# A new instruction order for an attention and mixer kernel, from a planner that counts two readers of one PSUM tile as serial, with the first loads on one queue

## The chip, the cores and the metric

The kernel runs on one core of one Trainium2 chip. The metric is the device time of one execution in microseconds (us). Every kernel ran at least four times, in rounds beside the kernel before on the same chip. A ratio of two kernels is the mean time of the one's fast runs over that of the other's fast runs of the same rounds, so it is not quite the ratio of the medians that stand beside it. The medians of the kernel before in the six sets of rounds, each on another chip or at another time, lay between 365.7 and 366.2 us; differences below are taken to the median of the same rounds.

Engine names in the profile: PE is TensorE's matmuls, PEld its weight loads, DVE VectorE, ACT ScalarE, POOL GpSimd, SP SyncE.

## The reference, cut to what matters

```python
# attention with random features: 8 batches x 8 heads, 576 tokens, head size 64
proj = einsum('bhsd,md->bhsm', x, omega)            # "angles"
phi  = concat([cos(proj), sin(proj)]) / sqrt(128)   # features, of q and of k
kv, z = phi(k)^T v, sum of phi(k)
attn = (phi(q) kv) / (phi(q) z)                     # "num", then "norm"
# mixer: u = x + low-rank mix over tokens (U, V), then an MLP of width 2048
out = u + relu(u @ w_ch1) @ w_ch2
```

The heads are worked on in 32 pairs; the MLP of a batch needs the four pairs of that batch. The MLP is the bulk of TensorE's work (W1 and W2, 128x512 matmuls); the features are the bulk of VectorE's (casts of angles out of PSUM, shifts by a quarter turn) and ScalarE's (sines).

## The kernel before

The program is a list of 1294 operations. A string ORDER, found by a search outside of the kernel, says in which order they are emitted (with a or b for the engine where two are possible), and SLOTS which buffer each takes. Every engine then runs its own instructions strictly in that order and waits where data or buffers are missing. The semaphores come from the framework, not from the plan; the plan's times are used in the kernel for one thing alone, the number of dummy matmuls ("fills") that are put in front of a TensorE operation in the first 36 us.

Two double-bank PSUM tiles, pp0 and pp1, carry angles, kv sums and numerators. One of them has two readers for each pair:

```python
tps = pair["tv"] if g else ps.pair()      # the tail angles of this pair go into ...
kvp = pair["tv"] = ps.pair()              # ... the tile that holds the previous pair's kv sums
...
o_tc  = add("tcp", "DVE", 0.34, ..., tensor_copy(tt..., tps.t[:, :, 256:384]))       # L652, "tail cast"
o_kvc = add("kvc", ("DVE", "ACT"), (0.34, 0.27), ..., copy(e, kvb, kvp.t[:, :, 0:130]))  # L797/L799, "kv copy"
```

The fills, and the first loads (om is omega, ld0 the first k and q; ScalarE issues omega and q, SyncE k, V and U):

```python
n = int((t - last - 0.15) / 0.09) if t < FILL else 0
...
o_om = add("om", "ACT", 0.5, -99, lambda _: nc.scalar.dma_start(om_f, omega), post=1.6)
for src, lo, e in ((k, NJ, "SP"), (q, 0, "ACT")): ...
    first.append(add("cast0", ("DVE", "ACT"), (0.36, 0.6), -98, cast, deps=[o_r], uses=[raw, qk]))
```

Of the kernel before, what the change touches and what calls it, by code (L numbers as in the profile page):

```python
# [11 lines left out]
ACT = mybir.ActivationFunctionType  # L12
# [11 lines left out]
NJ = 9  # L24
# [85 lines left out]
FILL = 36.0  # L110
# [9 lines left out]
19 0 11 10 20a 49 50 21 4 12 9 13 25 22a 27 77 14 28b 26a 23 8 78 29 106 51 53 32 30 33 35 6 105 55 31 54b 36 57  # L120
56b 81 37 34 59 39 60 58 38 79 173 7 82b 24 202 61 83 40 229 41 62 85 63 64 66 42b 84a 109 107 65 68 52 88 87 67
86 69 2 5 90 111 15 112b 174 43 70b 89 110a 91 95 44 71 113 72 257 94 116 114 258 117 93 80 230 73 92 97 74b 96 1
98b 3 201 175 17 119 120 108 121 45 115 118 46a 99 123 122 18 125 16 75 100 124 277 47 48b 126a 203 127 177 76a
101 179 128 207 102b 103 178b 129 180a 181 130a 182 205 176 184 185 187 233 208b 131 104b 206b 138 235 234b 278
231 132b 188 209 183 139 261 149 236a 259 140a 189 147 186 150a 145 190 262a 133 148a 212 210 193 1075 191 194b
338 339 281 237 213 215 146a 1073 216 240 211 192 263 264a 163 1074 155 214 157 164b 156a 217 195 218 204 141 159
219 158a 160a 232 238 1076 221 279 342 134b 222b 196 265 220 241 239 142b 244 242 135 153 154a 136 357 358 223 243
268 245 151 171 152a 249 260 224 246 266 250a 267 172a 280 269 376 197 225 137a 271 247 167 226a 395 248 161 168a
169 198b 270 251 199 162b 340 170b 143 165 273 272 144a 252 253 396 464 254b 200a 166b 282 361 377 275 255 274
256b 331 283b 1083 227 276 341 1084 359 329 378 228b 328 332 284 330 1085 333 334 1086 1087b 285 286 335 287a 343  # L130
288 1077 349 350 289b 1078 347 292 348 337 351 344a 322 1079 293b 310 323b 482 352 380 399 290 311a 353 502 1080
296 291a 297a 312 520 1081a 336 362 354 397 300 301a 313b 363b 463 367 369 366 320 355 360 321b 345 465 356 346
370 314 318 467 315a 371 326 483 364 372 368 589 319b 304 305a 1095 365 373 381 385 374 386 389 387 327a 382b 1096
1097 298 1098 388 1088 299b 375 383 391 607 390 379 484 324 392 294 1099b 325a 398 384 394 308 393 400 486 309b
454 626 455 302 456 453 295a 401b 457 461 458 306 402 303b 459 1089 316 460 403 466 317a 1090 1091 501 307b 1092
468 1093b 503 404 521 462 472 473 1113 405b 469b 406 407 1114 1094 414 415 627 1115 1116 470 485 477 504 1082 474
1117b 410 475 1100 471 476 480 478 411 1101 1102 1103 1104 487 646 1105b 416 479 488b 481 1107 433 492 505 413 522
491 495 489 494 496 493 490 408 434a 498 1108 1109 412 590 409 497 499 451 588 506 511 1110 500 513 512 524 609
507b 508 510 523 514 1111b 509 421 422a 628 452b 1118 515 516 1119 1120 437 517 1121 438b 592 713 525 526b 580 425
1106 518 579 578 647 426a 581 732 1122 519 608 582 1123b 439 445 446b 527 528 440a 591 610 583 447 441 448a 442b  # L140
419 420b 529 584 1124 593 597 429 530b 586 430a 611 645 443 714 599 751 535 1125 1126 444b 449 417 418a 450a 536
585 587 598 531 1127 629 770 538 532 427 428b 537 533 601 431 534 602 432a 594a 603 1128 423 435 1129a 539 595
424b 1130 436a 1131 1132 540 596 612 1112 630 600 605 604 613b 606 619 648 616 649 618 564 565b 1133 1134 733 574
771 617 621 546 620 575a 614 572 547a 1135 615 622 1143 573a 623 1144 625 631 636 1145 1146 624 637 632a 1147 554
555a 633 638 643 635 640 639 1137 634 570 566 567a 641 552 1138 571a 541 558 642 553b 650 717 704 706 736 559a 705
1139 1140 1141 1148 839 715 562 651b 857 703 707 734 644 563b 576 652 709 752 653 1149 1150 1151 654 577b 655a 708
718 724 722 550 1152 710 755 719b 716 753 735 725 551a 772 1136 877 1153 542 876 568 660 661 560 712 1161 663 723
895 711 664 665 666 726 543a 561a 569b 1162 727 720 729 728 556 964 731 656 544 548 549a 754 1163 840 662 1164 838
657 721 557a 737 545a 1165 1154 683 742 658 730 738b 741 746 745 743 747 1167 1168 1169 744 1170 756 659 748 1171
760 1155 1156 739 763 684a 774 679 858 1142 761 764 750 749 680a 762 740 673 765 687 688a 767 842 1157 757a 695  # L150
758 696a 1166 766 674b 861 681 1158 769 682a 759 775 1159 1173 880 1172 830 829 1174 776a 768 1160 667 1175 777
982 828 668a 983 1176 831 669 832 833 836 778 1177 670b 697 834 693 694a 773 698b 835 843 859 878 779 837 849 847
848 701 780b 702a 841 852 1179 699 789 851 850 844a 700a 896 899 1180 855 781 853 897 782 965 671 672a 854 790 677
675 676a 785 845 685 686a 689 678a 690a 1002 786 791 1181 1182 846 691 1183 862 867 963 866 870 692a 863b 826 784
868 869 1197 1198 1199 871 872 787 1200 860 873 856 827a 881 1201 1191 808 887 783 882b 1192 885 886 809b 874 788
864 888 875 883 865 889 1193 890 984 891 1184 814 818 815a 892 884 810 1194 819b 811b 893 879 900 812 1195 1215
894 956 813a 953 954 1003 804 955 1196 805b 957 901b 902 1202 898 822 823a 1216 1217 903 967 904 960 958 1218 905b
798 906 799a 959 1219 907 961 1001 794 824 968 795b 825a 966 975 974 802 820 1203 972 800 821b 796 797b 801a 910
1204 911 1205 973 803b 962 985 969a 976 978 1220 1206 908 792 793a 909 970 979 1207 977 806 816 914 807a 980 1185
915 1186 971 981 1187 1188 986 1189 912 913 987 817a 991 992 1005 1208 996 941 988b 994 995 993 1209 1210 1211 997  # L160
942b 921 1212 998 1006 1190 922a 1213 1010 943 1221 989 999 1000 1011 1013 1012 1014 990 1222 1007b 925 1015 1016
1008 944a 926a 1223 1018 1178 1017 1009 1224 1004 1225 927 1019 1020 928b 1233 947 1214 1021b 1022 1023 929 1234
948a 930b 937 938a 1024 1025b 931 932a 1235 1026 916 933 1030 1027 934a 919 1028 945 1031 923 924b 920a 946a 949
1236 950a 1033 1034 1029 939 1032 935 1237 1227 1228 936a 917 1229 1230 1037 940a 1043 1044a 918b 1055 1231 1038a
1035 1239 1056a 1047 1049 1039 1232 1048b 1226 1059 1060a 1240 1050a 1036 1241 1040a 1242 1243 1041 1061 1042a
1245 1246 1051 1062b 1052b 1238 1063 1064a 1071 1065 1247 1072b 1069 1070a 1248 1053 1054a 1045 1249 1066b 1046b
1251 1067 951 952b 1068a 1057 1252 1253 1250 1254 1269 1270 1058b 1255 1271 1257 1244 1272 1273 1263 1274 1258
1256 1259 1260 1275 1264 1276 1261 1281 1265 1277 1278 1262 1279 1280 1282 1266 1267 1283 1284 1268 1285 1287 1288
1289 1290 1286 1291 1293 1292
"""  # L170
SLOTS = """
001010200031011010101000112420500021001311100311100001112002102001301011022100100010020101012010212200100301203101
130011111021021202101211010100410000032101051020101200112101110101220110212310001020110200002211213003024110311000
122112221010005100001010112010321202010013121122000001121102103000000112130003200110212010013010011210101000221002
200310011310210100420200012010210130021215101201300211112111001010123221000120100002011021001011200120001010112211
012120101000102100232132031200101400111150203121100100100200101010010021001102112020110122031201010020200101312300
011100120000100120120120221100111100022010120002101012211120310210101312010001100021110103210100200211100122120013
21100113022000111002201002202110031000110102110100101120112002011220120121201001000101002001122010211
"""

LAT = {"PE": 0.21, "DVE": 0.14, "ACT": 0.16, "POOL": 0.2, "SP": 0.15}


class Plan:
    def __init__(self):
        self.ops = []

        self.rings, self.hw, self.landed = 0.0, 0.0, []

    def add(self, *a, **k):  # L190
# [132 lines left out]
    def follow(self, begin, switch=0.1):  # L323
# [3 lines left out]
        for i, k in words:  # L327
            o = self.ops[i]
            o.on, o.dur = o.eng[k], o.dur[k]
            for d in o.deps:  # L330
                d.users.append(o)
        free, ready, held = dict(begin), {}, {}
        mode = 0
        for i, _ in words:
            o = self.ops[i]
# [7 lines left out]
            if isinstance(o.post, tuple):  # L343
                o.post, dur = self.transfer(o, s, dur)
# [678 lines left out]
```

## Time and profile before

| | kernel before |
|---|---|
| time, median of 4 (range) | 365.69 us (365.07 to 366.57) |
| span in the profile, clock of TensorE | 364.7 us, 0.987 |
| first MLP matmul starts | 37.3 us |
| last matmul ends | 360.0 us |
| first angle cast starts (L650) | 7.1 us |
| fills | 93 |

Everything before the start of the first MLP matmul, "the head" below, produces the first batch's features; from then on TensorE has MLP work to do and is nearly always busy. A profile's span is one execution; the one shown of the kernel before took 366.4 us, near the upper end of its range. Its trace is therefore some 0.7 us worse than its median.

### The profile page before, as it was taken

To read this page: it belongs to the slowest core of one execution; us is meant where nothing else is said; L and a number is where in the kernel's file an instruction comes from. 1 tells how busy PE (TensorE), PEld (TensorE's weight loads), DVE (VectorE), ACT (ScalarE), POOL (GpSimd) and SP (SyncE) were. 2 spreads that over 40 slices of the span, in tenths; PEclk is the share of its full clock that TensorE was granted. 3 is DMA by queue.
4 is the path that set the end of the run, shared out by engine and by line. 5 is a ranking of instruction groups with operands and counts; after the bars stand their busy time and mean duration, and the time that the engine had idled before them with its cause. 6 is when DMAs were issued, how large, how long until landed. Compare 5 with 4: busy or idle time off the path is not lost.

```text
span 364.7 us, 9575 instructions
## 1 busy us (share of the span) xinstructions
PE 344.1 (94%) x4084; PEld 192.3 (53%) x4139; DVE 254.2 (70%) x415; ACT 214.7 (59%) x278; POOL 82.7 (23%) x146
## 2 busy tenths in 40 slices
PE   4969989998999999999999999999999999999994
PEld 2647556545555754455555555565444554455442
DVE  4887989868877888687788888689767833324221
ACT  3877999758775774577467678475546833131000
POOL 7892517233131152034300721000000000000000
PEclk9987999999999999999999999999999999999998
DMA  8999999998066965599746999413364102402034
GB/s 176 183 171 206 203 168 159 134 150 134 4 95 147 152 129 94 96 172 139 139 64 119 152 122 160 79 24 78 71 82 102 38 0 59 90 6 60 21 79 101
DMA packets 67067, 39.74 MB, mean 109 GB/s; under 512 B 46928, under 2 KB 61008, under 8 KB 67024
## 3 DMA queue, kind: packets, MB, share of 16 engines
q0 software_dynamic: 16704, 18.06, 35.0%
q1 hardware_dynamic: 49952, 20.61, 34.4%
q8 instruction: 32, 0.52, 0.6%
q10 hardware_dynamic: 368, 0.46, 0.4%
q14 instruction: 11, 0.09, 0.1%
HBM read 37.11 MB, written 9.44 MB: 128 GB/s over the span
## 4 chain that ended last, share of the span: by engine, by line
PE 87%; DVE 6%; ACT 2%; DMA 2%; issue 2%; POOL 0%; DVEq 0%; POOLq 0%
PE pb L913 32%; PE pb L858 29%; PE pp L698 6%; PE pb L877 4%; PE pp L713 4%; PE pp L825 2%; DMA qk<-in_q_dram 2%; PE pp L613 2%; PE pb L627 2%; PE pb L987 1%; DVE tt L650 1%; DVE x L728 1%; PE pb L589 1%; PE pp L719 1%; DVE cc L675 1%
## 5 line engine op out<-in xcount | busy, mean ns | idle before, releaser
L858 PE MATMUL pb<-uT,W1b 128*128 128x512 bf16 x488 | 121.4, 379 | 1.5 <-issue 0.3
L913 PE MATMUL pb<-W2b,hid 128*128 128x512 bf16 x489 | 120.3, 379 | 1.3 <-issue 0.3
L805 ACT ACTIVATE hid<-pb 128x512 bf16<-128x512 f32 x83 | 47.9, 595 | 62.4 <-PE pb L858 62.1
L679 ACT ACTIVATE f<-tt 128x1152 bf16<-128x1152 int16 (+1 forms) x64 | 74.1, 1162 | 13.9 <-DVE tt L652 6.0
L682 ACT ACTIVATE f<-cc 128x1152 bf16<-128x1152 int16 (+1 forms) x64 | 73.9, 1161 | 11.1 <-DVE cc L675 10.8
L913 PEld LDWEIGHTS <-hid 128*128 128x128 bf16 x512 | 48.3, 98 | 55.3 <-issue 2.0
L858 PEld LDWEIGHTS <-W1b 128*128 128x128 bf16 x512 | 47.7, 98 | 55.9 <-issue 3.6
L675 DVE TENSOR_SCALAR cc<-tt 128x1152 int32<-128x1152 int16 (+1 forms) x64 | 49.7, 780 | 1.4
L650 DVE CAST tt<-pp 128x1024 int32<-128x1024 f32 x32 | 38.9, 1217 | 5.1 <-PE pp L613 4.6
L803 DVE TENSOR_SCALAR hid<-pb 128x512 bf16<-128x512 f32 x45 | 30.6, 685 | 15.4 <-PE pb L858 14.8
L577 POOL COPY v<-vraw 128x576 bf16<-128x576 bf16 x32 | 22.6, 710 | 74.8 <-PE pp L620 31.7
L944 DVE TENSOR_TENSOR o<-pb,x 128x512 f32<-128x512 f32 x24 | 16.6, 690 | 29.8 <-PE pb L913 27.7
L659 DVE CAST tt<-pb 128x512 int32<-128x512 f32 x48 | 31.9, 684 | 5.1 <-PE pb L627 5.0
L549 POOL DMA_DIRECT2D qk<-in_k_dram x31 | 17.4, 560 | 54.7 <-DMA qkt<-qk 49.4
L728 DVE TENSOR_TENSOR x<-pp,rc 128x640 bf16<-128x640 f32 x32 | 26.4, 825 | 1.1
L549 POOL DMA_DIRECT2D qk<-in_q_dram x31 | 18.0, 585 | 34.7 <-DMA qkt<-qk 30.2
L698 PEld LDWEIGHTS <-f 64*128 64x128 bf16 x1152 | 20.0, 95 | 11.2 <-issue 4.2
L830 DVE TENSOR_TENSOR x<-pp,x 128x1024 bf16<-128x1024 f32 (+1 forms) x18 | 18.7, 1044 | 10.2 <-PE pp L825 9.9
L698 PE MATMUL pp<-v,f 64*128 64x65 bf16 x1152 | 23.6, 192 | 2.2 <-DVE tt L652 1.2
L713 PEld LDWEIGHTS <-f 128*128 128x128 bf16 x512 | 20.5, 99 | 7.5 <-issue 1.7
L713 PE MATMUL pp<-kvb,f 128*128 128x65 bf16 x512 | 21.8, 195 | 1.0 <-DVE tt L652 1.0
L652 DVE CAST tt<-pp 128x256 int32<-128x256 f32 x32 | 13.4, 419 | 12.8 <-ACT kvb L799 7.3
(79 smaller groups left out, 305.9 us busy)
## 6 DMA issues: line engine op xcount, KB each, us to landing
out_dram<-o SPq DMA_DIRECT2D x71, 128.0 KB, 2.5
vraw<-in_v_dram POOLq DMA_DIRECT2D x32, 144.0 KB, 6.8
qk<-in_k_dram POOLq DMA_DIRECT2D x31, 144.0 KB, 5.0
qk<-in_q_dram POOLq DMA_DIRECT2D x31, 144.0 KB, 5.5
W1b<-in_moe_w_ch_dram POOLq DMA_DIRECT2D x2, 1024.0 KB, 12.2
W2b<-in_moe_w_ch_dram POOLq DMA_DIRECT2D x4, 512.0 KB, 13.2
uT<-x SPq DMA_TRANSPOSE x30, 2.5
qkt<-qk SPq DMA_TRANSPOSE x24, 5.2
```

What stands on the lines that cost most here:

```text
L549: nc.gpsimd.dma_start(qk.t[:, lo:lo + NJ, :], src[b, 2 * hp:2 * hp + 2].rearrange("h (p j) d -> (h p) j d", j=NJ))
L650: o_kc = add("kcp", "DVE", 1.14, rank, lambda _: nc.vector.tensor_copy(i32(tt.t)[:, 1280:2304], kps.t.rearrange("p a b -> p (a b)")), deps ...
L659: nc.vector.tensor_copy(i32(tt.t)[:, 640 * lo:640 * lo + 512], t.t)
L675: nc.vector.tensor_scalar(out=i32(cc.t)[:, 0:n], in0=tt.t[:, lo:lo + n, 0], scalar1=16384.0, scalar2=None, op0=ALU.add)
L679: nc.scalar.activation(out=fe.t[:, 1, lo:hi], in_=tt.t[:, lo:hi, 0], func=ACT.Sin, scale=SIN_SCALE)
L682: nc.scalar.activation(out=fe.t[:, 0, lo:hi], in_=cc.t[:, 0:n, 0], func=ACT.Sin, scale=SIN_SCALE)
L698: nc.tensor.matmul(kvp.t[:, hh, 65 * s:65 * s + 65], fe.t[pr, s, 1152 + P * jj:1280 + P * jj], v65.t[pr, KJ[jj], :], start=(jj == 0), stop ...
L713: nc.tensor.matmul(nps.t[:, hh, 65 * i:65 * i + 65], fe.t[:, s, c0:c0 + 128], kvb.t[:, hh, s, :], start=(s == 0), stop=(s == 1))
L803: nc.vector.tensor_scalar(out=o, in0=i, scalar1=0.0, scalar2=None, op0=ALU.max)
L805: nc.scalar.activation(out=o, in_=i, func=ACT.Relu)
L858: nc.tensor.matmul(hp_.t, w1h[:, ct, fs], uT.t[:, ct, 0:512], start=(ct == 0), stop=(ct == NCT - 1))
L913: nc.tensor.matmul(d, w, W2b[c4][:, f % 4, :], start=(f == 0), stop=(f == NFT - 1))
```

## The change

Its intent: the planner that the search uses is told that two engines which read one PSUM tile do so one after the other; the order is searched again with it; omega, the first k and the first q go through SyncE's hardware queue, U and V behind them; the fills are reckoned with more margin.

```diff
-19 0 11 10 20a 49 50 21 4 12 9 13 25 22a 27 77 14 28b ...        (ORDER and SLOTS: all of it new)
+19 10 12 0 11 20a 49 9 13 14 50 77 78 25 21 22b 26a 29 ...
 ...
+                if isinstance(u.cls, Banks):
+                    s = max([s] + [e for on, e in read.get(u, {}).items() if on != o.on])
 ...
-                n = int((t - last - 0.15) / 0.09) if t < FILL else 0
+                n = int((t - last - 0.3) / 0.1) if t < FILL else 0
 ...
-    o_om = add("om", "ACT", 0.5, -99, lambda _: nc.scalar.dma_start(om_f, omega), post=1.6)
+    o_om = add("om", "SP", 0.43, -99, lambda _: nc.sync.dma_start(om_f, omega), post=1.35)
 ...
-            for src, lo, e in ((k, NJ, "SP"), (q, 0, "ACT")):
+            for n, (src, lo) in enumerate(((k, NJ), (q, 0))):      # both issued by nc.sync
```

22a became 22b: the first q is cast by ScalarE. In all, 100 operations change between VectorE and ScalarE, 50 each way. Lines move by 9: L652 is L661 in the changed kernel, L799 is L808, L858 is L867, L627 is L636. In spliced kernels below with the loads of before, they move by 6.

## The prediction

> **What bounds the kernel now.** I read the page's busy shares first, then the busy times stretch by stretch, then what TensorE waited for, then the chain of waits, and last the timeline of the first 38 us.
>
> The busy shares say "TensorE", at a clock that is nearly full (0.987):
>
> ```profile
> PE 344.1 (94%) x4084; PEld 192.3 (53%) x4139; DVE 254.2 (70%) x415; ACT 214.7 (59%) x278; POOL 82.7 (23%) x146
> ```
>
> An average hides the stages, so I cut the span into stretches (columns: length, then busy us and instruction count of PE, PEld, DVE, ACT, POOL, then granted clock, DMA share, GB/s):
>
> ```profile
> 0.00:9.10 9.10, 4.03 (x35) 2.65 (x36) 3.78 (x14) 3.49 (x5) 6.46 (x18) 1.00 0.86 175
> 9.10:18.20 9.10, 8.66 (x126) 6.33 (x124) 7.51 (x10) 8.02 (x10) 7.52 (x15) 1.00 1.13 183
> 18.20:36.50 18.30, 14.55 (x306) 11.63 (x307) 14.80 (x29) 14.05 (x19) 11.06 (x19) 0.81 1.11 189
> 36.50:80.00 43.50, 41.16 (x586) 24.32 (x591) 37.82 (x61) 36.32 (x51) 16.55 (x28) 1.00 1.24 160
> 80.00:120.00 40.00, 38.20 (x550) 22.42 (x558) 31.23 (x51) 28.39 (x36) 11.37 (x21) 1.00 0.59 100
> ...
> 200.00:240.00 40.00, 39.54 (x478) 21.23 (x484) 31.55 (x52) 27.45 (x35) 10.73 (x18) 1.00 1.01 125
> ```
>
> There are three stages. From 36.5 us to 355 us TensorE is the bound: adding the stretches, it is idle 6.6 us of 318.5. 4.1 of those lie before 120 us; after that there is about 0.5 us in each 40. Before 36.5 us TensorE is not the bound, whatever its digits say: part of its 27 busy us are matmuls on the identity that only fill holes (93 of them, all before 33.5 us), and it idles 9.3 us besides. After 360.0 us there is only a tail: last matmul, a 0.69 us add, the store, the end.
>
> The first MLP matmul starts at 37.3 us. What delays it is the production of the first batch's features on VectorE and ScalarE: I added the measured durations of VectorE's instructions in program order up to the fourth normalisation, 26.6 us, and the trace ends that one at 35.6 us. So VectorE lost 9.0 us, of which 3.6 are the wait for the first load, and most of the rest is named by these lines (waits before VectorE, then before TensorE):
>
> ```profile
> DVE tt L661 <- PE pp L627: 2.4, 2, 1.4
> DVE tt L652 <- ACT kvb L799: 1.1, 1, 1.1
> DVE tt L650 <- PE pp L613: 1.0, 1, 1.0
> ...
> PE pp L613 <- DVE x L728: 1.9, 1, 1.9
> PE pp L698 <- DVE tt L652: 1.2, 1, 1.2
> PE pb L589 <- DMA qk<-in_q_dram: 0.8, 1, 0.8
> ```
>
> "tt L652 <- ACT kvb L799" is the subject of the change: both instructions READ the same pp tile (L799 copies the kv sums, L652 the tail angles, in other columns), and each waits for the other. Over the run it happens 6 times one way (7.3 us of VectorE) and 8 times the other way (6.3 us of ScalarE). The planner inside the kernel, whose order was searched, did not know of it.
>
> **What the Trainium skill says.** (1) "PSUM — Partial Sum Buffer", section "PSUM bank collisions raise a hardware error": two engines touching the same bank and quadrant must be ordered, ScalarE and VectorE reads of it included. The trace agrees that the two readers are ordered, with the 7.3 and 6.3 us above; no run shows the error. The wait is therefore not removed by the change, only made known to the search. (2) "DMA: Bandwidth & Descriptors", section "Issuing engines are not separate DMA queues": loads issued by several engines share the 16 DMA engines, and spreading them saves only issue time. The trace fits: the first q, issued by ScalarE at 1.17 us beside SyncE's k, V and U, took 4.0 us, k 3.3. (3) "TensorE: Matmul & The Clock Gate", section "What's actually happening": the clock falls to half after an idle window of some 3.4 us. Here it falls to 0.5 for about 24 to 31 us, after a 1.9 us hole at 22.2 to 24.1; so the trace shows the fall, but after a hole shorter than that alone.
>
> **The change part by part.**
>
> *Loads.* ScalarE's two issues (0.39 and 0.45 us) go to SyncE; the built order there is k, omega, q, then U, then V (not omega first). In the kernel before, VectorE casts k at 4.03 to 4.49, then stands 0.71 us for q and casts it in 0.46, and only then copies WT (5.57) and the transposed k (5.71); angles of k follow at 6.47 and their cast at 7.12. In the changed order ScalarE casts q, so VectorE gets back 1.17 us; but the k transposes end at 5.15 on TensorE, so the copy can move only from 5.71 to about 5.2: 0.5 us. Omega, now behind k, comes no sooner than 1.17 + 2.8 = 4.0 us, and its cast stands ahead of k's: minus 0.15. k alone at the head of the queue should land a little sooner: plus 0 to 0.3. **Sum: +0.4 us** at the first angle cast.
>
> *The second pair's q (GpSimd queue).* Before, it is issued at 1.96, lands at 8.58, and the angles of the first q wait behind it in TensorE's order until 9.59. In the new order it is issued after the identity is made, so at about 2.8, and now both the tail angles and the q angles stand behind its transposes. With 6.6 us again it lands at 9.4 and costs 0.7; with the 5.5 us median of its kind it lands at 8.3 and gains 0.3. V and U start later, which speaks for the shorter one. **Sum: 0 us, between -0.7 and +0.6.**
>
> *Order up to the first MLP matmul.* Work does not change in kind: VectorE's sum up to the fourth normalisation is 25.9 us instead of 26.6 (same durations, new order), ScalarE's up to the third u copy 27.7 instead of 27.5. So only holes can go. After the first q angle cast (10.24) VectorE's holes up to 35.6 are 2.4 us: 25.4 elapsed less 23.0 of work. The largest is the 1.13 us behind ScalarE's kvb copy at 20.7, then 1.44 behind L627 at 29.6. If the known reader conflict and the smaller gaps go by half, that is 1.2, and 0.7 less work ahead of that point, of which I count 0.3, since ScalarE does not get less. **+1.4 us.**
>
> *Fewer fills.* The formula wants 0.3 us more margin and 0.1 us each: 62 instead of 93 (counted in the built order). On the clock of a hole this is free; it takes away fills that overran (the chain holds fill pieces of 1.17 and 1.06 us), but leaves holes that may pull the clock down. I count **+0.2**.
>
> *Order after that.* TensorE's real work is the same 4046 matmuls. Waits that the profile gives to a VectorE reader are 1.9 us after 36.5 us (L627 1.4, L713 0.5), other named ones 1.5. Against that the row-tiling of TensorE changes 106 times instead of 101. I expect the search to recover 0.8 of the 6.6 idle us and lose 0.3 to switches: **+0.5.** Work moves from ScalarE to VectorE (4 relu, 2 kvb copies, 2 output copies, 2 qkt copies: about ten instructions at 0.4 to 0.7 us, 6 us of VectorE), which has 70% of the span in use, so it is hidden beside TensorE.
>
> *Tail.* Both orders end with a W2 tile, an add on VectorE and two half stores: 0.
>
> Sum: 0.4 + 0 + 1.4 + 0.2 + 0.5 = 2.5 us. Everything gained before 37 us moves the start of a TensorE-bound stage, so it should come through at full value; 365.5 - 2.5 = **363.0 us**.
>
> **Rivals.** *The load takes the place of the wait*: the second pair's q lands at 9.4 or later, blocks the tail and q angles together, and the head gains nothing; then only the later terms count, 363.5 to 364.5. For it: the issue is surely later, and the planner is optimistic about this load. Against it: the queue ahead of it is lighter by V. *VectorE and ScalarE are the bound of the head anyway*: their work before the first MLP matmul is 26 and 28 us and is almost unbroken from 10 us on, so a better order only exchanges one hole for another; 364.5 to 365.5. For it: the holes are only 2.4 us. Against it: the measured reader conflict is real and sits in that stretch. *The clock*: 31 fewer fills leave a longer hole and half clock lasts longer, or the reverse, the hole at 22 us disappears and with it some 3 us of half speed in work that stands on the chain (L698 took 1.17 instead of 0.72 us, L713 1.06 instead of 0.67): 1 us either way, 362.0 or 364.0. *The order is fitted to a model*: any real duration that the model has wrong opens a new TensorE wait in the middle; 366 is then possible.
>
> **Range and chances.** TensorE's idle time, 20.6 us in all, with about 3.7 us before its first possible matmul and 4.8 us of tail, leaves some 12 us to gain at all, and faster by over 2% would need 7.3 of them: I give it 0.03. Slower by 2% would need new holes larger than all those now in the middle stage: 0.02. The range takes the best of the first two and the clock term (361.2) and, above, a head that gains nothing and a middle stage that gives back a little (365.4).
>
> **What would show it.** Right: q cast on ScalarE, the first angle cast at about 6.7 instead of 7.12; first MLP matmul at 35 to 36 us; VectorE's wait on ScalarE's kvb copy and the reverse down from 7.3 and 6.3 us to a half; TensorE idle between 36.5 and 355 at about 6 us. Wrong: the second pair's q landing after 9.4; the fourth normalisation still at 35.6; a granted clock in 18 to 36.5 us that is well below 0.81; or a wait of TensorE in the middle that was not there.

## The result, and the profile after

The changed kernel takes **360.18 us** (359.98 to 361.04), against 365.69: 5.5 us less, ratio 0.9852 (95% interval 0.9825 to 0.9878). The predicted 363.0 and its range (361.2 to 365.4) were too slow: the direction was right, the size was half.

First the page's line of busy time, then the same stretches as in the prediction (columns: length; busy us and count of PE, PEld, DVE, ACT, POOL; clock; DMA share; GB/s), of the changed kernel:

```profile
PE 341.8 (95%) x4051; PEld 189.5 (53%) x4108; DVE 257.2 (72%) x423; ACT 210.4 (59%) x270; POOL 84.9 (24%) x146
```

```profile
9.10:18.20 9.10, 8.58 (x167) 6.27 (x163) 8.99 (x14) 8.87 (x11) 7.98 (x15) 1.00 1.21 220
18.20:36.50 18.30, 15.26 (x265) 10.62 (x267) 16.81 (x29) 16.33 (x24) 12.14 (x21) 0.91 1.16 207
36.50:80.00 43.50, 42.42 (x661) 25.50 (x669) 39.35 (x68) 37.99 (x51) 18.75 (x32) 1.00 1.22 171
80.00:120.00 40.00, 39.58 (x577) 23.03 (x581) 31.75 (x53) 26.53 (x32) 5.70 (x9) 1.00 0.54 86
```

Read the DVE column: 8.99 of 9.1 us and 16.81 of 18.3, where it was 7.51 and 14.80. From 36.5 to 120 us TensorE's idle time went from 4.1 to 1.5 us. Beyond 120 us little is left to compare: some 0.5 us in each 40 before and after, and even that is not real (below).

The first MLP matmul now starts at 33.7 us (37.3). So I cut both traces there, and ended the cut at the last matmul. Kernel before, then the changed one:

```profile
37.29:359.98 322.69, 316.08 (x3611) 170.98 (x3663) 226.58 (x364) 188.54 (x246) 56.85 (x96) 1.00 0.67 101
```

```profile
33.67:353.57 319.90, 316.08 (x3605) 170.42 (x3659) 229.87 (x373) 184.50 (x237) 60.28 (x97) 1.00 0.65 103
```

TensorE is busy for the same 316.08 us in both; the stretch is 2.8 us shorter, which shows as idle time alone: 6.6 us became 3.8. Some 3.5 us of both figures are no idle time. In each of the two traces more than 50 matmul records are missing: over the run they hold 4084 matmuls for 4139 weight loads, and 4051 for 4108. Two later traces that lack none, e10_earlynorm (the old order but for two operations in the head) and e12_unswap (the new order but for six turned pairs), show the same stretch:

```profile
34.83:357.53 322.70, 319.81 (x3665) 171.03 (x3663) 226.59 (x364) 188.56 (x246) 58.54 (x98) 1.00 0.64 102
```

```profile
33.58:353.51 319.93, 319.39 (x3661) 170.34 (x3659) 229.50 (x373) 184.19 (x237) 59.53 (x97) 1.00 0.63 103
```

There TensorE is idle for 2.9 us in the old order and 0.5 in the new one, and between 120 and 320 us for less than 0.1 in either. So the new order removed nearly all the idle time that there was.

The head is 3.6 us shorter. Together that is 6.4 of the 6.5 us by which the two profiled spans differ; about 0.9 of it is the choice of runs, since the one profiled of the kernel before was 0.7 us above its median and that of the changed kernel 0.2 below.

The head, from the first angle cast to the end of the fourth normalisation, kernel before and changed kernel:

```profile
7.12:35.63 28.51, 23.53 (x422) 18.27 (x422) 23.57 (x38) 22.55 (x29) 17.97 (x31) 0.88 1.12 188
```

```profile
6.21:32.11 25.90, 21.63 (x392) 16.16 (x393) 23.56 (x38) 23.27 (x29) 18.06 (x33) 0.93 1.17 209
```

VectorE does 38 instructions in 23.57 and in 23.56 us. Nearly the same work (one copy of u less, one of transposed q and k more) takes 28.5 us in one order and 25.9 in the other: VectorE's idle time fell from 4.9 to 2.3 us. Both traces lie at the long end of their kind. Over the same stretch e4, e6 and e8, which have the old head, take 26.4 to 27.2 us with 2.8 to 3.4 idle; e2, e3, e5 and e19, which have the new one, take 24.4 to 25.1 with 1.4 to 1.8 idle. So the usual difference is some 2 us, 1.5 of it VectorE's idle time. What ended its idle time there in the changed kernel (the lines of before stand in the prediction, save two smaller ones of 0.6 and 0.5 us):

```profile
DVE pp L735 <- PE pp L728: 0.9, 1, 0.9
DVE qkt L806 <- PE pb L598: 0.8, 1, 0.8
DVE tt L659 <- PE pp L622: 0.7, 1, 0.7
DVE tt L670 <- PE pp L636: 0.4, 1, 0.4
```

Over the whole run VectorE's wait on ScalarE's kv copy went from 7.3 us to nothing, and ScalarE's wait on the tail cast from 6.3 to 4.3 us. In the kernel before three of the six waits reached TensorE after the head. These are all the waits of TensorE that the profile names after its first MLP matmul, before and after:

```profile
PE pp L627 <- DVE tt L652: 1.4, 2, 0.7
PE pp L698 <- DVE x L728: 0.6, 1, 0.6
PE pp L713 <- DVE tt L652: 0.5, 1, 0.5
PE pb L913 <- issue: 0.5, 3, 0.2
PE pb L784 <- DVE x L728: 0.4, 1, 0.4
PE pb L858 <- issue: 0.3, 2, 0.2
```

```profile
PE pp L707 <- issue: 0.5, 1, 0.5
PE pb L922 <- issue: 0.3, 2, 0.2
PE pb L867 <- issue: 0.2, 1, 0.2
```

Every named wait of TensorE on VectorE is gone from this stretch. That is a finding on the order as a whole. Which part of the change did it, a comparison of two traces cannot say.

### The profile page after: what moved, and what is told of

Read it like the earlier page. It is cut to its first block, busy times and chain, and to the rows that moved or that the text cites. A ratio compares the mean times of both kernels' runs of the same rounds, so it can differ in the third digit from the quotient of the medians.

```text
span 358.2 us, 9506 instructions
## 1 busy us (share of the span) xinstructions
PE 341.8 (95%) x4051; PEld 189.5 (53%) x4108; DVE 257.2 (72%) x423; ACT 210.4 (59%) x270; POOL 84.9 (24%) x146
## 4 chain that ended last, share of the span: by engine, by line
PE 90%; DVE 4%; issue 2%; ACT 1%; DMA 1%; SPq 0%; DVEq 0%
PE pb L922 35%; PE pb L867 31%; PE pp L707 6%; PE pb L886 4%; PE pp L722 4%; PE pp L622 2%; PE pp L834 2%; PE pb L636 1%; DMA tt<-in_q_dram 1%; PE pp L728 1%; PE pb L793 1%; DVE cc L684 1%; DVE tt L659 1%; DVE x L737 1%; DVE tt L670 1%
## 5 line engine op out<-in xcount | busy, mean ns | idle before, releaser
L867 PE MATMUL pb<-uT,W1b 128*128 128x512 bf16 x490 | 122.4, 379 | 1.3 <-issue 0.2
L922 PE MATMUL pb<-W2b,hid 128*128 128x512 bf16 x487 | 119.1, 379 | 1.6 <-issue 0.3
L867 PEld LDWEIGHTS <-W1b 128*128 128x128 bf16 x512 | 47.6, 98 | 55.6 <-issue 3.6
L814 ACT ACTIVATE hid<-pb 128x512 bf16<-128x512 f32 x79 | 46.1, 594 | 40.9 <-PE pb L867 40.7
L812 DVE TENSOR_SCALAR hid<-pb 128x512 bf16<-128x512 f32 x49 | 33.1, 686 | 20.8 <-PE pb L867 20.8
L586 POOL COPY v<-vraw 128x576 bf16<-128x576 bf16 x32 | 23.5, 738 | 80.9 <-PE pp L629 47.8
L555 POOL DMA_DIRECT2D qk<-in_k_dram x31 | 19.1, 616 | 40.7 <-DMA qkt<-qk 39.6
L737 DVE TENSOR_TENSOR x<-pp,rc 128x640 bf16<-128x640 f32 x32 | 26.4, 825 | 1.1
L555 POOL DMA_DIRECT2D qk<-in_q_dram x31 | 17.3, 560 | 33.3 <-DMA qkt<-qk 29.9
L585 POOL DMA_DIRECT2D vraw<-in_v_dram x32 | 18.3, 575 | 5.2 <-DMA qk<-in_k_dram 1.8
```

The source lines that it names most:

```text
L555: nc.gpsimd.dma_start(qk.t[:, lo:lo + NJ, :], src[b, 2 * hp:2 * hp + 2].rearrange("h (p j) d -> (h p) j d", j=NJ))
L812: nc.vector.tensor_scalar(out=o, in0=i, scalar1=0.0, scalar2=None, op0=ALU.max)
L814: nc.scalar.activation(out=o, in_=i, func=ACT.Relu)
L867: nc.tensor.matmul(hp_.t, w1h[:, ct, fs], uT.t[:, ct, 0:512], start=(ct == 0), stop=(ct == NCT - 1))
L922: nc.tensor.matmul(d, w, W2b[c4][:, f % 4, :], start=(f == 0), stop=(f == NFT - 1))
```

## The experiments

All outputs are right.

| run | edit | median us | before beside it | ratio (95% interval) |
|---|---|---|---|---|
| e1_loads | before + new loads | 368.37 | 365.94 | 1.0066 (1.0045 to 1.0087) |
| e2_order | changed, loads of before | 360.02 | 365.94 | 0.9836 (0.982 to 0.9853) |
| e3_oldfill | changed, old fill formula | 359.14 | 365.94 | 0.9823 (0.9805 to 0.9842) |
| e4_newfill | before + new fill formula | 365.72 | 365.94 | 1.0005 (0.9983 to 1.0026) |
| e5_newhead | new order up to the MLP, old after | 362.86 | 365.78 | 0.9918 (0.99 to 0.9936) |
| e6_newrest | old order up to the MLP, new after | 362.52 | 365.78 | 0.9904 (0.9861 to 0.9946) |
| e7_swap | before, six reader pairs swapped | 363.27 | 365.78 | 0.9937 (0.9909 to 0.9965) |
| e8_heavyfill | before, 191 fills | 365.20 | 365.78 | 0.9979 (0.9952 to 1.0006) |
| e10_earlynorm | before, first num and norm earlier | 365.15 | 365.95 | 0.9998 (0.9963 to 1.0033) |
| e11_both | e7 and e10 together | 364.66 | 365.95 | 0.9966 (0.9932 to 1.0) |
| e12_unswap | changed, six reader pairs put back | 360.27 | 365.95 | 0.9847 (0.9831 to 0.9863) |
| e13_best | e3 + six more pairs swapped | 362.37 | 365.95 | 0.9903 (0.9887 to 0.9918) |
| e14_castact | before, first q cast by ScalarE | 366.63 | 366.15 | 1.0011 (0.9998 to 1.0024) |
| e15_vwork_new | changed + 3.0 us of VectorE work | 362.78 | 365.91 | 0.9919 (0.9887 to 0.995) |
| e16_vwork_old | before + the same work | 370.26 | 365.91 | 1.0122 (1.009 to 1.0153) |
| e17_awork_new | changed + 3.0 us of ScalarE work | 362.86 | 365.91 | 0.9914 (0.9876 to 0.9952) |
| e18_splice | new order up to some 62 us, old after | 362.74 | 365.91 | 0.9916 (0.9884 to 0.9947) |
| e19_best | e3 with the loads of before | 359.82 | 366.15 | 0.9826 (0.9813 to 0.9839) |

### Which of the four parts: loads, order, fills

The diff has parts that can be taken one by one: ORDER and SLOTS are only strings over the same list of operations, and either string builds with either set of loads.

```diff
 e1_loads = kernel before with
+    o_om = add("om", "SP", ...nc.sync...)          and the new loop for the first k and q
 e2_order = changed kernel with
+    o_om = add("om", "ACT", ...nc.scalar...)       and the old loop
```

> The kernel before with the new load section alone (omega and first q on SyncE, k then omega then q, V and U behind; old order of everything else, q still cast on VectorE). Theory A (the gain is the order): within 1 us of before, about 365 us, since VectorE still stands for q in front of the copies that the first angles need; first MLP matmul at 36.5 to 37.5 us in its trace. Rival B (the loads carry the head): at least 1.5 us faster, first MLP matmul at or below 35.8 us. A half: the first q lands later than before (5.2 us), as it did in the changed kernel (6.3 us), and then it is slower than before by up to 1 us.

> The changed kernel with the old load section (omega and first q issued by ScalarE, here behind its table load, as the new order has it). Theory A: most of the 5.5 us stays, 360 to 361.5 us, first MLP matmul at 33.5 to 35 us. Rival B: the gain falls below 3.5 us, over 362.2 us. The second part of the gain, TensorE's idle time after the first MLP matmul (6.7 us before, 3.9 us after), must stay at about 3.9 us under both.

Measured: the loads alone make the kernel 2.4 us *slower*; the order without them keeps the whole gain (5.9 us in its rounds). The half of e1's expectation that I had put last was the right one. When the cast of the first q starts, in the kernel before, in e1_loads and in the changed kernel:

```profile
5.20 0.46 DVE L797 CAST qk<-tt 128x576 bf16<-128x576 f32 x1 [0.71 <-DMA tt<-in_q_dram]
```

```profile
7.58 0.46 DVE L800 CAST qk<-tt 128x576 bf16<-128x576 f32 x1 [2.88 <-DMA tt<-in_q_dram]
```

```profile
6.30 0.67 ACT L808 CAST qk<-tt 128x576 bf16<-128x576 f32 x1 [4.07 <-DMA tt<-in_q_dram]
```

The bracket is the idle time of the engine ahead of the instruction. Behind k and omega on one queue, q comes 1.1 to 2.4 us later than from ScalarE's queue. In the old order (e1, first MLP matmul at 39.9 us) VectorE stands for it, with the first angles' copies behind it. In the new order ScalarE stands for it, and has nothing else to do yet. **So the new loads are no part of the gain; the new order makes them harmless.**

```diff
 e3_oldfill = changed kernel with                 e4_newfill = kernel before with
+n = int((t - last - 0.15) / 0.09) ...            +n = int((t - last - 0.3) / 0.1) ...
```

> The changed kernel with the old fill formula: 100 identity matmuls instead of 62. If the fills matter through the time that they take: slower by 0.5 to 1.5 us (the chain of the kernel before held fill pieces of 1.2, 0.9, 1.0 and 1.1 us). If through the clock (half speed from about 24 to 27 us in the changed kernel): faster by up to 1 us, clock above 0.97 in 18 to 36 us. If neither: within 0.4 us of 360.2.

> The kernel before with the new fill formula alone: 62 identity matmuls instead of 93. As a cost of time: faster by 0.5 to 1.5 us, first MLP matmul at 36 to 36.8 us. Through the clock: slower, with half speed for longer than the 7 us of before. If neither: within 0.4 us of before.

e4 shows no difference (365.72, interval across 1). e3 ran at a clock of 0.998 to 1.000 in its four runs and at 359.14 us, where e2 in the same rounds took 360.02; their intervals overlap. So in the order of before fewer fills cost and bring nothing; in the new order more fills hold the clock and are worth at most about 1 us, which the runs do not settle.

### Where in the order: two splices

Both orders emit nearly the same set of operations ahead of the first MLP matmul (155 and 158, seven differ), so they can be cut there and joined crosswise, with PSUM slots chosen so that nothing live collides.

```diff
 e5_newhead: ORDER = [first 158 operations of the old order, in the sequence of the new one] + old order from there
 e6_newrest: ORDER = [first 155 operations of the new order, in the sequence of the old one] + new order from there
```

Both have the loads of before and the new fill formula.

> A splice: everything that the kernel before orders ahead of its first MLP matmul, but in the new order; after that the old order word for word. Loads by the old section, new fill formula. Theory A (two independent gains, 3.6 us before the first MLP matmul and 2.8 us after it): 362 to 362.8 us, first MLP matmul at 33 to 34.5 us, TensorE idle after it about 6.5 us as before. Rival B (the early start is used up, because the old order then waits for VectorE and ScalarE): over 364 us with the first MLP matmul just as early and more than 8 us of idle after it. Rival C (the middle is the cause and the head only follows): not faster than 365.

> The opposite splice: the operations that the new order has ahead of its first MLP matmul, in the old order; after that the new order word for word. Theory A: 362.5 to 363.5 us, first MLP matmul at 36.5 to 37.5 us, idle after it about 3.9 us. Rival B: 361 or less, the late start is partly made good. Rival C: below 361.5. If A holds, the gains of the two splices add up to that of the whole order (5.9 us).

e5 is 2.9 us faster than before, e6 3.3; the sum, 6.2, is the 5.9 us of e2 within their scatter (e6's four runs lie between 360.9 and 363.9). In the traces the first MLP matmul starts at 33.8 us (e5) and 35.6 (e6), and from there to the last matmul it takes 322.8 us (e5, as before) and 320.8 (e6; 319.9 in the changed kernel). e6's start is earlier than theory A said; e4 and e8, with the old head and other fills, show 35.6 and 35.8 as well, so 37.3 was a late case of the old head. **By the clock theory A stands: the part of the order up to the first MLP matmul and the part after it are worth about 3 us each, and they add up.** Rivals B and C fall as they were stated.

Where the new head's 3 us become visible is less sharp. e4 and e8 start the MLP 1.7 and 1.5 us earlier than the trace of the kernel before, but end their last matmul only 0.6 and 0.5 us earlier: TensorE then has one more wait (L698, 0.9 and 0.8 us). Against these two, e5 gains some 1.9 us ahead of its first MLP matmul and 0.9 after it. An early start is not always kept.

### The readers of one PSUM tile

```diff
 e7_swap: in the order of before, six times
-... kvc(ScalarE, pair g)  tcp(VectorE, pair g+1) ...
+... tcp(VectorE, pair g+1)  kvc(ScalarE, pair g) ...
```

> The kernel before with six pairs of readers of one PSUM tile swapped in the order and nothing else: where VectorE's tail cast waited for ScalarE's kv copy (7.3 us in six places), the tail cast comes first. Theory A1 (the readers' wait is what the new order removes): VectorE's wait on the kv copy goes from 7.3 to 0, TensorE's waits on the tail cast (1.9 us after 36.5 us, 1.6 before) mostly go, and the time falls by 2 us or more, to 363.5 or less. Rival A2 (the wait is only one of many and off the path, or the other reader pays instead): less than 1 us, with ScalarE's wait on the tail cast rising from 6.3 us.

2.5 us less by the medians, 2.3 by the ratio. VectorE's wait on the kv copy is 0 (7.3 before), ScalarE's on the tail cast 7.7 (6.3). In the trace of before three waits of TensorE followed directly on such a wait (the first three lines; the fourth, a wait on a normalisation, comes 7 us after the third). The same stretch of e7 has two (kernel before first; columns: start, duration, instruction, idle time before it and what ended it):

```profile
43.93 0.39 PE L627 MATMUL pp<-qkt,WT 64*128 64x512 bf16 x2 [0.64 <-DVE tt L652]
51.34 0.39 PE L627 MATMUL pp<-qkt,WT 64*128 64x512 bf16 x2 [0.74 <-DVE tt L652]
83.61 0.67 PE L713 MATMUL pp<-kvb,f 128*128 128x65 bf16 x16 [0.55 <-DVE tt L652]
90.29 0.73 PE L698 MATMUL pp<-v,f 64*128 64x65 bf16 x36 [0.64 <-DVE x L728]
```

```profile
42.83 0.39 PE L627 MATMUL pp<-qkt,WT 64*128 64x512 bf16 x2 [0.70 <-ACT kvb L799]
50.98 0.40 PE L613 MATMUL pp<-WT,qkt 64*128 64x128 bf16 x8 [1.72 <-DVE x L728]
```

At 83 and 90 us the waits are gone for good. At 43 us the wait is as long as before and only names the other reader; at 51 us another took its place. So A1 holds in part: by the clock the six swaps are worth some 2.4 us in the old order. My reading is that a swap helps only where the engine that is made to wait has time. The trace cannot settle it: e7's profiled run is the slowest of its four by 1.5 us (364.87; the others 362.88 to 363.34), its stretch after the first MLP matmul is only 0.5 us shorter than before, and its start of the MLP, 36.2 us, lies within what the old head shows. Where the 2.4 us are gained stays open.

Now the converse, and the same in places where the new order has the kv copy first:

```diff
 e12_unswap: changed order, six times:  tcp ... kvc  ->  kvc tcp
 e13_best:   changed order, six other times:  kvc tcp  ->  tcp kvc;  old fill formula
```

> The converse of e7: the changed kernel with six pairs of readers put back the wrong way round (ScalarE's kv copy ahead of VectorE's tail cast, where the new order had the cast first and little in between). Theory A1: VectorE's wait on the kv copy comes back (0 in the changed kernel, 3 us or more here), and the time rises by 0.7 to 2.5 us to 360.9 to 362.7. Rival A2 (the order as a whole is good, no single pair of readers matters): within 0.4 us of 360.2.

> A try for a better version: the changed kernel with the old fill formula (e3: 359.1 us) and the six remaining places where ScalarE's kv copy stands directly ahead of VectorE's tail cast swapped. The trace of the changed kernel shows no wait of VectorE on these copies, so theory A1 says that there is nothing left to win by them: 358.8 to 359.5 us. If waits on readers still cost something that the profile does not name: 358.5 or less.

e12 falls to the rival: VectorE's wait on the kv copy came back, 3.4 us in four places, and the time did not move (ratio 0.9847, against 0.9852 of the changed kernel in its own rounds). e13 is worse than either theory allowed: 3 us slower than e3, by ratios of 0.9903 and 0.9823. What the two traces say of the readers, e12 and then e13:

```profile
DVE tt L661 <- ACT kvb L808: 3.4, 4, 1.5
```

```profile
ACT kvb L808 <- DVE tt L661: 13.8, 11, 2.3
```

In e13 ScalarE's wait on the tail cast grew from 4.3 to 13.8 us, and TensorE waits once, at 131.7 us, 0.73 us for a kv copy, which it never did there before. After its first MLP matmul e13 takes 321.4 us, e3 319.4. **Neither reader should go first as a rule.** Which one may wait depends on who stands behind it, and that is what a planner can only weigh if it knows of the wait. My theory A1 in its simple form, "the wait is the loss, remove it and gain", is refuted.

### What bounds the head

```diff
 e8_heavyfill: kernel before,  n = int((t - last) / 0.06)
 e10_earlynorm: order of before, num of pair 0 directly behind tr of pair 3, norm of pair 0 directly behind kcp of pair 2
 e11_both: e10 and e7
```

> The kernel before with a fill formula that fills all it can: 191 identity matmuls instead of 93, to hold the clock. Clock theory (half speed from 24 to 31 us is a cause of the late head): clock above 0.97 in 18 to 36 us, L698 and L713 in their full-speed durations there, first MLP matmul 1 to 2 us earlier, 364 to 365 us. Rival (VectorE and ScalarE set the head; or the fills themselves are in the way): 365.5 or more.

> The kernel before with two operations moved and nothing else: the first pair's numerator matmuls right behind its kv copy and the third pair's first transposes, and its normalisation right behind the third pair's first angle cast, as the new order has them. Both PSUM pair tiles are then not held by two numerators at once. Theory H1 (the head's gain is the PSUM pair tile that comes free earlier): TensorE's wait of 1.9 us on the normalisation at 24 us goes, first MLP matmul at least 1 us earlier than in the same order without it (35.6 to 37.3 us were seen), 1 us or more off the time, 364.8 or less. Rival H2 (the sum of VectorE's work in the head decides, so moving it about does nothing): within 0.6 us of before.

> The two moves of e10 and the six swaps of e7 together in the kernel before. If they are independent: 2.3 us of e7 plus what e10 brings, some 362 to 362.8 us, more than half of the whole 5.6 us. If both remove the same wait: no better than e7, 363.3 us.

(Pairs are counted from 0.) e8 holds the clock at 0.998 to 1.000 and starts the MLP at 35.8 us, but gives 0.6 us with an interval that crosses 1. A full clock bought with 98 more fills is worth at most some 1.8 us by that interval; the fills themselves did not make the kernel slower, so TensorE has room in the head. e10 removed the wait that it was made to remove (1.9 us of TensorE at 24 us), and no gain is shown: ratio 0.9998, with an interval of 1.3 us to either side. Its four runs lie between 364.0 and 367.1, and the profiled one is the fastest of them, so its trace, with the first MLP matmul at 34.8 us, must not be taken for the kernel. That favours H2, but H1's 1 us is not excluded. e11 (0.9966) is not better than e7 alone (0.9937, in other rounds); its interval and that of e7 overlap.

The head's 2.9 us had no single wait to its name. The remaining theory was the sum (theory V): VectorE is the bound there, and any idle time of it is lost.

```diff
 e15_vwork_new, e16_vwork_old (VectorE's shift, pairs 1 and 2, twice with the same result)
-    nc.vector.tensor_scalar(out=i32(cc.t)[:, 0:n], in0=tt.t[:, lo:lo + n, 0], scalar1=16384.0, ...)
+    for _rep in range(2 if g in (1, 2) else 1):
+        nc.vector.tensor_scalar(out=i32(cc.t)[:, 0:n], in0=tt.t[:, lo:lo + n, 0], scalar1=16384.0, ...)
 e17_awork_new (ScalarE's sine, pairs 1 and 2)
+    if g in (1, 2):
+        nc.scalar.activation(out=fe.t[:, 1, lo:lo + 760], in_=tt.t[:, lo:lo + 760, 0], func=ACT.Sin, ...)
```

> The changed kernel with more work for VectorE in the head and nothing else: the four angle shifts of the second and third pair are each done twice (4 x 0.75 = 3.0 us; the result is the same). Theory V (VectorE is the bound of the head, and what the new order did was to take idle time out of it: 28.5 us with 23.6 busy before, 25.9 with 23.6 busy now): at least 2.2 of the 3.0 us arrive in the time, 362.4 or more, first MLP matmul at 36 us or later. Rival (the chain through loads, TensorE and ScalarE sets the head): less than 1.2 us.

> The same 3.0 us of extra VectorE work in the kernel before, whose VectorE stands idle for 4.9 us in the head (2.3 in the changed kernel). Theory V, holes as slack: part of it is absorbed in the holes, the time rises by 0.5 to 2 us, to 366.3 to 367.8, less than in the changed kernel. If the holes are no slack but waits in the chain itself (each ends when work that VectorE did earlier comes back): it rises by the full 2.2 to 3.0, as in the changed kernel.

> The changed kernel with as much more work for ScalarE in the head: four sines of the second and third pair get a second pass over 760 columns (4 x 0.75 = 3.0 us, same result). ScalarE is busy 23.3 of 25.9 us there, so theory V with some slack on ScalarE says less than in the VectorE case: plus 0.3 to 1.8 us. If both engines are equally the bound: 2.2 us or more, as for VectorE.

3.0 us more for VectorE cost the changed kernel 2.6 us (median 362.78 against 360.18 of other rounds; 2.4 by the difference of the ratios). The same 3.0 us for ScalarE cost 2.7 (2.3 by ratios). In e15 the first MLP matmul starts at 35.7 us, a little before the 36 that I had asked for. So VectorE bounds the head, but not alone: ScalarE does as much, and theory V's "some slack on ScalarE" is wrong. They work in a chain (cast, shift, sine, and by way of TensorE the kv copy and the normalisation), each nearly full. In the kernel before the 3.0 us cost 4.4. The head of e16, then of e15 (the first cut ends 0.4 us before the fourth normalisation does, the second 0.9 us after it):

```profile
7.10:38.00 30.90, 23.40 (x421) 18.60 (x420) 26.35 (x41) 22.27 (x28) 21.21 (x35) 0.78 1.15 194
```

```profile
6.20:35.00 28.80, 23.21 (x414) 17.56 (x413) 26.71 (x44) 23.67 (x31) 22.18 (x37) 0.82 1.18 207
```

Over the exact stretch VectorE is idle 4.5 us in e16 and 2.0 in e15, against 4.9 and 2.3 in the traces without the work (1.4 to 3.4 in their other traces): of 3.0 us the holes took up 0.5 at most. **A hole of a full engine in such a chain is not slack.** My explanation, which no run tests by itself, is that a hole ends when something comes back that the engine itself had delivered earlier, so more work delays both. Why e16 lost 4.4 us and not 3.0 stays open: TensorE's clock was also lower there (0.78 in the head, 0.88 before), and no run separates the two.

### The start, and the second half of the gain

```diff
 e14_castact: order of before, 22a -> 22b (first q cast by ScalarE)
 e18_splice: [first 278 operations of the old order, in the sequence of the new one] + old order from there
 e19_best: changed kernel, loads of before, old fill formula
```

> The kernel before with the first q cast by ScalarE instead of VectorE and nothing else: the one piece of the new head that the prediction gave a number (VectorE gets 1.17 us back, the copy of the transposed k moves from 5.71 to 5.2 us, the first angle cast from 7.12 to about 6.6). If a half microsecond at the start of the chain arrives at the end: 365.0 to 365.4 us, first angle cast at 6.6 us. If it is caught by the next wait (the second pair's q, which held the first q angles until 9.6 us): first angle cast at 6.6 us and no change in the time, 365.6 to 366.

> A second splice, further on: the first 278 operations of the old order (up to about 62 us) in the new order, then the old order word for word; loads of before, new fill formula. With the new order up to the first MLP matmul alone it was 362.9 us, with all of it 360.0. If the second part of the gain is made where VectorE and ScalarE are still over 90% busy (37 to 60 us: TensorE idle 1.8 us there before, 0.9 after): 360.8 to 362. If it is made later (60 to 100 us: 2.0 against 0.4): 362.3 or more.

> A try for the best version: new order, loads of before, old fill formula. The old fills gave the changed kernel 359.1 us with the clock full throughout, the old loads left it at 360.0. If the two are independent: 358.6 to 359.2 us. If the old fills only helped because they hid the late first q: 359.8 to 360.4.

e14: no gain (1.0011), and the first angle cast did not come at 6.6 us but at 7.68, later than before. VectorE was indeed free earlier, its copy of the transposed k starts at 5.24; but TensorE's order has a burst of fills and the transposes of q ahead of the k angles:

```profile
4.99 1.81 PE L987 MATMUL pp<-ident 128*128 128x128 bf16 x15
6.59 0.71 PE L589 MATMUL pb<-ident,qk 128*128 128x128 bf16 x5
7.24 0.40 PE L613 MATMUL pp<-WT,qkt 64*128 64x128 bf16 x8
```

Its plan gave the slower cast on ScalarE more time, and the formula filled that time: 106 fills in all instead of 93. One engine's gain at the start needs the other's order to go with it; the new order has the k angles ahead of the q transposes.

e18 is inconclusive. At 362.74 us it is no better than e5, which by the letter says that the second gain is made after 62 us. But its trace shows the gain made early and lost at the seam: TensorE is busy for all of 36.5 to 50 us (12.76 of 13.5 before, in a trace that lacks records), and then waits where the old order takes over:

```profile
57.45 1.02 PE L864 MATMUL pb<-uT,W1b 128*128 128x512 bf16 x4 [0.69 <-ACT hid L811]
59.56 0.45 PE L704 MATMUL pp<-v,f 64*128 64x65 bf16 x18 [0.49 <-ACT f L685]
```

The whole traces say it more simply. Over the first 22.7 us after the first MLP matmul TensorE is idle 1.8 us before and 0.9 after; over the next 40 us, 2.0 and 0.4. That is 2.5 of the 2.8 us. In the traces without missing records (e10 and e12) it is 1.3 and 0.5, then 1.6 and 0.

e19 at 359.82 does not add the two small things up. No version was found that beats the changed kernel beyond doubt: e3 has the lowest median (359.14), but its ratio and that of the changed kernel, 0.9852, have overlapping intervals.

## Why the prediction was right or wrong

Right: which stage bounds what; that the tail and the work of TensorE stay; that a gain ahead of the first MLP matmul arrives in full, for the new head (e5: 3.4 of 3.5 us in the trace), though not in e4 and e8; that the readers' waits fall to a half or less (13.6 us in all to 4.3); that the fills matter little; that it is faster by less than 2%. The two half store streams at the end and the 4046 real matmuls are unchanged, as it said.

Wrong, by its own terms:

- **"Order up to the first MLP matmul", +1.4 us. This is one of the two steps that failed**, by size: e5 measures 2.9. The step took VectorE's holes as 2.4 us, of which half would go. First, a slip, visible in its own lines: the two largest holes that it names, 1.13 and 1.44 us, already exceed 2.4. 25.4 us less "23.0 of work" counted the work ahead of the first q angle cast too low; with the durations that the step used it is 26.6 - 4.4 = 22.2, and the holes are 3.2. Second, I started counting at 10.24 us and left the holes before it to the loads. From the first angle cast on, the holes are 4.9 us, and 2.6 of them went (some 3.1, and 1.5 of them, in the other traces). Also 1.2 and 0.3 make 1.5, not 1.4. The rival that VectorE and ScalarE bound the head "anyway" had its premise right (e15, e17) and its conclusion wrong: here an order that removed VectorE's idle time was worth 2.9 us, and 1.5 to 2.6 us of that is seen as such idle time.
- **"Order after that", +0.5 us. The other step that failed**: again by size: the stretch after the first MLP matmul gained 2.8 us in the trace, e6 3.3 by the clock. I took 0.8 of 6.6 idle us, counted 3.4 us of named waits (the lines above add up to 3.7), and took off 0.3 for five more tiling changes. More than half of the 6.6 us were missing records and could not be won; of the 2.9 us that were real (e10), nearly all went, and the named waits fell from 3.7 to 1.0. So the named waits were the right thing to add up, and a quarter of them was the wrong share to take.
- "Loads", +0.4 us: wrong in sign by themselves (e1: 2.4 us slower) and 0 in the new order (e2). The step saw q stand behind k, and did not follow that to its landing: 6.3 us for 5.2. The first angle cast did come earlier, 6.21 us against 7.18 in e2, which has the same order with the loads of before; but the first MLP matmul did not (33.7 and 33.2), so the gain at that cast, which the step priced, was not carried on. e14 shows that the 1.17 us given back to VectorE are worth nothing under TensorE's old order.
- "The second pair's q", 0: in the changed kernel its transposes run in one burst with those of the first q, from 7.03 to 8.70 us, without a wait for that load; before, they started at 8.63 us after a wait of 0.79. So the first q angles came 0.6 us earlier (9.03 for 9.59), the good end of the step's range. No run separates it from the rest of the order.
- "Fewer fills", +0.2: 0 (e4).

What stays open: whether the new rule of the planner found this order, or a longer search would have found as good a one without it. The order was made outside of the kernel, and no run can tell. e7 shows that the rule concerns a real cost of 2.3 us in the old order; e12 and e13 show that in the new order such pairs can be turned with no change or with a loss.

## What to carry to other kernels

Where two engines in a chain are each some 90% busy and set the pace of a third, add up their idle time over the whole stage, from the first instruction of the chain on, and treat it as time that a better order may win: here it was not slack, about half of it went, and single waits taken out by hand won 2.4 us at best (e7), or moved. Before reading idle time of TensorE, compare the counts of matmuls and weight loads: over half of what looked idle here was missing records. Split a re-searched order by splicing old and new at a stage's edge before explaining it; here that gave two gains of 3 us that no comparison of two traces could have proved. And when a load goes behind others on one queue, look at when its reader starts, not at when it is issued.

## What the Trainium skill lacked or had wrong

- "DMA: Bandwidth & Descriptors", section "Issuing engines are not separate DMA queues", says that issuing from several engines only saves the issue time. For the landing of one load that was too little here: moved from ScalarE's queue to third place on SyncE's, the first q was issued 0.5 us later (1.67 for 1.17 us) and its cast started 1.1 us later in the changed kernel and 2.4 us later in e1, and e1 was 2.4 us slower as a whole. No run separates the shared queue from the third place in it.
- "TensorE: Matmul & The Clock Gate", section "What's actually happening", gives an idle window of about 3.4 us before the clock halves. In the kernel before it was at 0.50 from 26 to 30 us after a hole of 1.9 us, in the changed kernel at 0.50 from 24 to 26 us after holes of 1.4 and 0.3 us; in e3, with nearly as much idle time at the same place, it stayed at 1.00. In e17 it fell after a hole of 1.7 us and stayed at 1.00 after one of 2.05 us (27.9 to 29.9 us). A single hole's length does not decide.
- "PSUM — Partial Sum Buffer", section "PSUM bank collisions raise a hardware error", is right that two readers of one bank must be ordered, and says nothing of what that costs. Here VectorE waited up to 2.3 us for ScalarE's reader, six times in a run, and swapping the six was worth 2.3 us in the old order, while turning six such pairs in the new one changed nothing.
